# Spectral-mix kernel after sliding-window attention: the last mode's transposed rows by products with stationary weights, another order of the first units, and two weight packs cut into 112 and 8 partitions

## The chip, the core and the metric

The kernel runs on one core of a Trainium2 chip. The metric is device time in microseconds, the median of several runs. Five engines work side by side: PE (TensorE, matrix products; PEld is its weight load), DVE (VectorE), ACT (ScalarE), POOL (GpSimd) and SP (SyncE). Data moves through 16 DMA engines. DMAs that POOL issues form queue q0, those that SP issues form queue q1. What a DMA engine has in one queue it does in the order of issue. A DMA's rows are spread over the DMA engines, and a DMA counts as landed when the last of its engines has reported.

## The reference

```python
def _attn_ref(q, k, v):            # 8 batches, 8 heads, 576 tokens, 64 wide
    scores = scale * q @ k^T + bias (ALiBi slopes), masked to a causal window of 128
    return softmax(scores) @ v
def _moe_ref(x, w_r, w_i, w_ch):   # x: the attention's output as (8, 576, 512)
    X = rfft(x, axis=1); Xr, Xi = first 64 modes
    Yr = Xr @ w_r[m] - Xi @ w_i[m]; Yi = Xr @ w_i[m] + Xi @ w_r[m]
    u = x + irfft(Y, n=576)
    return u + relu(u @ w_ch)
```

The weights w_r and w_i are 64 matrices of 512x512 each in 4-byte floats, 134 MB in all. They are read once and cast to bf16 by the DMA itself.

## The kernel before

**Attention** fills the first 125 us. It leaves the tokens `x`, the spectra `XC` (channels in the partitions) and the table of the inverse transform `FT`.

**Modes.** Work is then ordered by mode. For each mode there are two weight tiles, numbered t = 2m (w_r) and t = 2m+1 (w_i), and each has four slices a of 128 rows. The product at line 886 holds 32 columns of `XC` stationary (8 batches, real and imaginary, with gaps) and lets a weight slice of 512 columns move: out come 32 rows of 512, in a quarter of the PSUM tile `acc`. Four modes are one quad g; g = 15 is the last (`LAST`). Its modes 60 to 62 go to a tile of their own, `part_acc` ("pa" in the profile), and mode 63 goes to the fourth quarter of `acc`.

**Weight stream.** POOL issues the weights (`load_w`, line 472; `load_packs`, line 491) into a ring of buffers, a pack of two tiles at a time: 128 partitions, 1 MB after the cast. The last packs come as single tiles (line 499), and the very last tile, t = 127, in three parts: slices 0 and 1, slice 2, slice 3. POOL's DMAs take turns at eight semaphores; each waits until the DMA eight places before it has landed, and a pack also waits until PE has used the buffer up.

**Beside the stream** PE turns spectra back into token space (`stream_spectra`, `project`, `augment`), at line 934 it runs `warm` products that nobody reads, and in the last quad, at i = 6, it begins unit 0 (`begin`, `channels`, `add_tokens`, `finish_tokens`). A unit is two batches by 128 tokens, or four batches by the last 64 tokens; there are 18.

**After the stream** stands an order written out by hand (lines 951 to 998). ACT scales mode 63's rows into `yq` in two halves (line 960), PE transposes them (962), DVE copies them to `yT` (964), PE multiplies `yT` by `w_ch` into `zl` (601), and ACT casts that to `yw` (603). DMAs then put the rows of quad 15 where the other units read them: `patch` (line 648) copies rows of `yq` to `Z` and of `yw` to `ZW`, per batch, batches 0 and 1 through SP or POOL and the others through POOL, eight rows each or six and two. Unit 0, and the channel half of unit 1, do not wait for these DMAs: they add the last quad's rows by a product with a small matrix `FM` (`last_rows`, line 786). `FM` is filled by two DMAs of 8 rows (line 916), early in the stream, between two packs.

For each unit the PSUM tile `mm` is the channel product, `yy` the tokens plus spectral rows; ACT takes the relu of `mm` (line 802), DVE adds `yy` (line 842; unit 0: lines 816 and 823) and SP stores the result (line 844). Five output buffers rotate.

Lines that the steps touch: 491 (packs), 593/596 (transposed rows of modes 60 to 62), 601/603, 648, 786, 816/823, 842, 886, 916, 955 to 998.

Of the kernel before, what the change touches and what calls it, by code (L numbers as in the profile page):

```python
# [412 lines left out]
def kernel(  # L413
# [46 lines left out]
    turns[1].remove(1)  # L460
    wq, homes, todo_w, again = {}, {}, [i for turn in turns for i in turn], []

    def load_w(n, pool, chosen=None):
# [11 lines left out]
    def load_packs(n, pool):  # L475

        for _ in range(n):
            pack = [i for i in todo_w if i not in again][:2]
            if not pack:
                return  # L480
            assert len(pack) == 2
            t = pool.tile([P, 2, 4, DM], BF16, tag="w", name="w")
            kinds = {i % 2 for i in pack}
            for s, i in enumerate(pack):
                todo_w.remove(i)
                homes[i] = pool if s else False
                wq[i] = [t[:, s, a] for a in range(4)]
            m, w = pack[0] // 2, (moe_w_r, moe_w_i)
            if len(kinds) == 1:
                assert pack[1] == pack[0] + 2  # L490
                nc.gpsimd.dma_start(  # L491
                    out=t.rearrange("p s a e -> p s (a e)"),
                    in_=w[kinds.pop()][m : m + 2].rearrange("m (p a) e -> p m (a e)", a=4))
                continue
            for s, i in enumerate(pack):
                src = w[i % 2][i // 2].rearrange("(p a) e -> p a e", a=4)
                for part in ((slice(0, 4),) if i < 2 * NM - 1
                             else (slice(0, 2), slice(2, 3), slice(3, 4))):
                    nc.gpsimd.dma_start(out=t[:, s, part], in_=src[:, part])
# [70 lines left out]
    with ExitStack() as mctx:  # L570
# [7 lines left out]
        nc.gpsimd.memset(YT[:, 1, :, :, HM - 4 :], 0.0)  # L578
        lctx, pctx = ExitStack(), ExitStack()
        lps = lctx.enter_context(tc.tile_pool(name="lps", bufs=1, side="right", space=PSUM))  # L580
# [17 lines left out]

        def late_channels(zw, yT, yw, c):
            for et in range(4):  # L600
                nc.tensor.matmul(zw[:, c], lhsT=yT[:, et], rhs=wch[:, et, c],
                                 start=(et == 0), stop=(et == 3))
            nc.scalar.copy(yw[:, c], zw[:, c])

# [131 lines left out]
        HALVES = (1, 2, len(units) - 1)  # L736
        mms, yys, rs = {}, {}, {}

# [73 lines left out]

        def with_tokens(o, n):

            last_rows(yys[0][0], 0, heads["yq"], (n,))
            nc.scalar.copy(o[:, n], yys[0][0][:, n])

        def finish_first(o):

            (mm, mm_slot), (_, yy_slot) = mms.pop(0), yys[0]  # L820
            for n in range(2):
                last_rows(mm, 0, heads["yw"], (n,))
                nc.vector.scalar_tensor_tensor(out=o[:, n], in0=mm[:, n], scalar=0.0,
                                               in1=o[:, n], op0=ALU.max, op1=ALU.add)
                nc.sync.dma_start(out=out[n, :P], in_=o[:, n])
                if n == 0:
                    with_tokens(o, 1)
            del yys[0]
            idle.append(mm_slot)
            free.append(yy_slot)  # L830

        def finish(j):

            b, st = units[j]
            if j not in yys:
                take(j)
            add_tokens(j)
            finish_tokens(j)
            (yy, slot), r = yys.pop(j), rs.pop(j)
            o = heads["out"].tile([P, 2, DM], FP32, tag="o", bufs=5, name="o")  # L840
            for c in parts(j):
# [8 lines left out]
                for n in range(c.start, c.stop):  # L850
# [3 lines left out]
                    )  # L854
            free.append(slot)

        quads, side, recycle = [], [], list(again)
        ZW = Z = XW = FM = FC = pairs = wch = w2 = None
        K1 = spot[again[-1]]
        for g in range(NM // 4):  # L860
# [5 lines left out]
            for i in range(8):  # L866
                k = 8 * g + i
                if i == 6 and g == LAST:
# [4 lines left out]
                    idle.append(0)  # L873
                    free.append(0)
                    begin(0)
                    channels(0)
# [4 lines left out]
                for a in range(4):  # L881
                    for t in now:
                        m, ri = t // 2, t % 2
                        c0 = (a // 2 * 2 * NC + 16 * (1 - ri) + a % 2 * 8) * NM + m
                        into = part_acc if g == LAST and m < NM - 1 else acc
# [13 lines left out]
                if k == K1:  # L899
# [14 lines left out]
                    nc.gpsimd.memset(FM, 0.0)  # L914
                    for b in range(2):
                        nc.gpsimd.dma_start(
                            out=FM.rearrange("(k v) b s -> k v b s", v=16)[:, b, b],
                            in_=FT[64 * b + 56 : 64 * b + 64, b, : 2 * P],
                        )
                    FC = right.tile([P, P], BF16, name="FC")  # L920
# [16 lines left out]
            if g < LAST:  # L937
                quads.append(quad_end(acc, g))
                next(quads[0])
            if g == 7:  # L940
                side += [partial(stream_spectra, 0, bp) for bp in range(B // 2)]
# [3 lines left out]
            elif g == LAST - 1:  # L945
# [5 lines left out]
        yq, yT = heads[LAST]  # L951
        zctx = ExitStack()
        zps = zctx.enter_context(tc.tile_pool(name="zps", bufs=1, space=PSUM))
        zl = zps.tile([P, DM], FP32, tag="z0", name="zl")
        nc.tensor.matmul(zl, lhsT=ident, rhs=wch[:, 0], start=True, stop=True)
        sides = (slice(0, DM // 2), slice(DM // 2, DM))
        trs = (lps.tile([P, 4, P], BF16, tag="tr", name="tr"),
               zps.tile([P, 4, P], BF16, tag="z1", name="tr1"))
        for i, c in enumerate(sides):
            nc.scalar.mul(yq[96:, c], acc[96:, c], 2.0 / S)  # L960
            for et in (2 * i, 2 * i + 1):
                nc.tensor.transpose(trs[i][:, et, 96:], yq[96:, et * P : (et + 1) * P],
                                    ident[96:, 96:])
            nc.vector.tensor_copy(yT[:, 2 * i : 2 * i + 2, 96:],
                                  trs[i][:, 2 * i : 2 * i + 2, 96:])
        patch([(nc.sync, 0), (nc.gpsimd, 1)], yq, lambda b: Z[:, b // 2, 1])
        patch([(nc.gpsimd, b) for b in (2, 3, 4, 5, 6)], yq, lambda b: Z[:, b // 2, 1], 6)
        yw = F[:, : DM // (2 * NM)].rearrange("p a b -> p (a b)")
        heads.update(yq=yq, yw=yw)
        first = heads["out"].tile([P, 2, DM], FP32, tag="o", bufs=5, name="o")  # L970
        with_tokens(first, 0)
        for i, c in enumerate(sides):
            zl = zps.tile([P, DM], FP32, tag=f"z{i}", name=f"zl{i}")
            late_channels(zl, yT, yw, c)
        zctx.close()
# [10 lines left out]
        channel_rows = partial(patch, rows=yw, dst=lambda b: ZW[:, b // 2, 1])  # L986
        channel_rows([(nc.sync, 0), (nc.sync, 1)] + [(nc.gpsimd, b) for b in range(2, B)])
        patch([(nc.gpsimd, 7)], yq, lambda b: Z[:, b // 2, 1], 6)

# [3 lines left out]
        finish(1)  # L993
        activate(2)
        for j in range(3, len(units)):
            activate(j)
# [32 lines left out]
```

## Time and profile before

| | us |
|---|---|
| median of 3 runs | 438.93 (438.69 to 439.68) |
| the profiled execution's own time | 437.99 |
| its span, first to last instruction | 436.1 |
| last weight matmul ends (line 886) | 402.8 |
| first output store issued (line 825) | 406.89 |
| last output store issued (line 851) | 430.80 |

| stretch, us from the span's start | what runs |
|---|---|
| 0 to 125 | attention; the first weights |
| 125 to 402.4 | weight stream, a pack each 4.9 us |
| 402.8 to 409.8 | mode 63's way to the first units |
| 409.8 to 436.1 | the remaining units, and their stores |

How to read it: the page gives each engine's busy time; the chain follows the end back from what released what; the timeline lists instructions with the idle time before them in brackets and what ended it. The trace also keeps, for each DMA, the times at which its 16 engines reported, and the start of every packet; where the text speaks of a DMA engine, it speaks of those.

### The profile page before, as it was taken

How to read it: one execution, taken by the hardware profiler on the slowest of the kernel's cores; microseconds unless marked ns; L12 is line 12 of the kernel's file. 1: busy time of each engine (PE TensorE's matmuls, PEld its weight loads, DVE VectorE, ACT ScalarE, POOL GpSimd, SP SyncE). 2: the span in 40 equal slices, each digit the busy share in tenths (PEclk: the TensorE clock that was granted, in tenths of full speed). 3: DMA queues.
4: the chain of work that ended last, by engine and by line, in shares of the span. 5: the costliest groups of instructions: out<-in, count | busy, mean ns of one | idle time of the engine just before them, and what ended most of it. 6: DMA issues, size and time to landing. Idle time of an engine off the chain costs nothing.

```text
span 436.1 us, 8292 instructions
## 1 busy us (share of the span) xinstructions
PE 316.2 (73%) x3488; PEld 177.7 (41%) x3509; DVE 184.5 (42%) x332; ACT 162.3 (37%) x211; POOL 90.2 (21%) x170
## 2 busy tenths in 40 slices
PE   5589899979686635543442487999889999788982
PEld 4367677757565312111111133444434444334430
DVE  7789799887783301000000021322213233122684
ACT  6949899988681000000000011322222322102780
POOL 8701010103424002222112110101111110012600
PEclk9969999999999955555555569999999999989997
DMA  8999999999999999999999999999999999998598
GB/s 285 326 311 310 290 316 300 307 298 299 252 217 212 215 215 213 214 214 214 215 212 214 214 215 214 215 214 215 215 214 214 215 215 215 213 215 153 190 378 311
DMA packets 50453, 105.54 MB, mean 242 GB/s; under 512 B 4032, under 2 KB 21072, under 8 KB 50416
## 3 DMA queue, kind: packets, MB, share of 16 engines
q0 software_dynamic: 19440, 68.41, 77.9%
q1 hardware_dynamic: 30976, 36.60, 25.3%
q8 instruction: 27, 0.44, 0.4%
q14 instruction: 10, 0.08, 0.1%
HBM read 162.53 MB, written 9.44 MB: 394 GB/s over the span
## 4 chain that ended last, share of the span: by engine, by line
DMA 71%; PE 10%; DVE 8%; issue 5%; POOL 2%; ACT 1%; SPq 1%; DVEq 0%; POOLq 0%; ACTq 0%
DMA w<-in_moe_w_i_dram 42%; DMA wch<-in_moe_w_ch_dram 8%; DMA qr<-in_q_dram 7%; DMA vr<-in_v_dram 6%; DVE o L842 3%; DMA qr<-in_moe_w_i_dram 3%; PE my L702 2%; DMA vr<-in_moe_w_r_dram 2%; DMA kr<-in_k_dram 2%; DVE vb L246 1%; PE acc L886 1%; PE av L344 1%; POOL Z L648 1%; PE my L659 1%; DVE att L318 1%
## 5 line engine op out<-in xcount | busy, mean ns | idle before, releaser
L886 PE MATMUL acc<-w,XC 128*32 128x512 bf16 x456 | 80.3, 478 | 68.5 <-DMA w<-in_moe_w_i_dram 34.2
L886 PEld LDWEIGHTS <-XC 128*32 128x32 bf16 x508 | 38.4, 147 | 109.2 <-issue 82.8
L307 ACT ACTIVATE att<-sc 128x1024 bf16<-128x1024 f32 x64 | 64.1, 1032 | 9.7 <-PE sc L297 9.6
L636 ACT CAST ZW<-zw 128x512 bf16<-128x512 f32 x8 | 4.7, 585 | 142.9 <-PE zw L634 142.9
L344 PE MATMUL av<-vb,att 128*128 128x132 bf16 (+1 forms) x576 | 38.4, 217 | 13.3 <-DVE x L360 8.6
L344 PEld LDWEIGHTS <-att 128*128 128x128 bf16 x704 | 36.6, 98 | 18.7 <-DVE x L360 12.0
L608 DVE TENSOR_SCALAR yq<-acc 128x512 bf16<-128x512 f32 x14 | 9.6, 687 | 81.8 <-PE acc L886 81.8
L702 PE MATMUL my<-wch,xT 128*64 128x512 bf16 x288 | 34.5, 381 | 5.7 <-ACT x L733 4.2
L711 ACT CAST XW<-my 128x512 bf16<-128x512 f32 x36 | 19.3, 589 | 50.5 <-PE my L659 50.5
L683 DVE COPY xT<-tr 128x1024 bf16<-128x1024 bf16 x18 | 12.4, 692 | 54.9 <-PE tr L681 54.9
L269 ACT COPY qkT<-tp 128x1152 bf16<-128x1152 bf16 x30 | 33.5, 1116 | 4.1 <-PE tp L263 3.6
L491 POOL DMA_DIRECT2D w<-in_moe_w_r_dram x22 | 15.6, 710 | 72.1 <-PE acc L886 46.1
L491 POOL DMA_DIRECT2D w<-in_moe_w_i_dram x23 | 16.3, 709 | 64.1 <-PE acc L886 45.3
L297 PE MATMUL sc<-qkT 64*64 64x256 bf16 (+2 forms) x640 | 25.1, 263 | 4.8 <-ACT qkT L269 1.2
L360 DVE TENSOR_TENSOR x<-av,rec 128x640 bf16<-128x640 f32 x32 | 26.4, 825 | 1.1
L702 PEld LDWEIGHTS <-xT 128*64 128x64 bf16 x288 | 17.1, 109 | 21.5 <-issue 9.1
L246 DVE CAST vb<-vr 64x1024 bf16<-64x1024 f32 x32 | 22.6, 708 | 0.2
L733 ACT CAST x<-my 128x512 bf16<-128x512 f32 x18 | 10.5, 585 | 31.6 <-PE my L659 31.6
L297 PEld LDWEIGHTS <-qkT 64*64 64x64 bf16 x640 | 14.5, 109 | 19.1 <-issue 16.0
L734 DVE CAST x<-my 128x512 bf16<-128x512 f32 x18 | 12.4, 692 | 21.7 <-PE my L659 21.7
L842 DVE TENSOR_TENSOR o<-yy,r 128x1024 f32<-128x1024 f32 (+1 forms) x20 | 20.3, 1059 | 2.1 <-ACT r L802 1.9
L318 DVE TENSOR_TENSOR att<-att,mask 128x1024 bf16<-128x1024 bf16 x32 | 20.5, 682 | 0.0
(137 smaller groups left out, 424.7 us busy)
## 6 DMA issues: line engine op xcount, KB each, us to landing
w<-in_moe_w_i_dram POOLq DMA_DIRECT2D x23, 1024.0 KB, 36.2
w<-in_moe_w_r_dram POOLq DMA_DIRECT2D x22, 1024.0 KB, 35.6
qr<-in_q_dram SPq DMA_DIRECT2D x16, 576.0 KB, 7.9
kr<-in_k_dram SPq DMA_DIRECT2D x16, 576.0 KB, 7.9
w<-in_moe_w_r_dram POOLq DMA_DIRECT2D x16, 512.0 KB, 14.2
vr<-in_v_dram SPq DMA_DIRECT2D x56, 128.0 KB, 7.6
w<-in_moe_w_i_dram POOLq DMA_DIRECT2D x13, 512.0 KB, 24.0
out_dram<-o SPq DMA_DIRECT2D x13, 512.0 KB, 5.0
```

The costliest lines, as they stand in the source:

```text
L246: nc.vector.tensor_copy(self.vb[u % 2][row, :, :, :, W * half : W * half + D], src[row, :2])
L269: (self.nc.vector.tensor_copy if u < 2 and w == "q" else self.nc.scalar.copy)(dst.rearrange("q h (p j) -> q h p j", j=TPP), tp.rearrange(" ...
L297: nc.tensor.matmul(sc[64 * half : 64 * half + 64, e, j * 256 + c0 : j * 256 + c0 + n], lhsT=qkT[row, 1, h, k0 + j : k0 + P : 2], rhs=qkT[r ...
L307: self.nc.scalar.activation(self.att[u % 2][:, kt * 8 * P : (kt + 1) * 8 * P], sc.rearrange("p e n -> p (e n)"), AF.Exp, scale=1.0 / math. ...
L318: nc.vector.tensor_tensor(out=rows, in0=rows, in1=self.table[:, heads], op=ALU.mult)
L344: nc.tensor.matmul(bank[:, qt * W : qt * W + rhs[j].shape[1]], lhsT=att[:, o : o + P], rhs=rhs[j], start=(n == 0 and j == 0), stop=(n == l ...
L360: nc.vector.tensor_tensor(out=self.x[:, b, :, cs].rearrange("p t (h d) -> p h t d", h=2), in0=tiles[:, :, :, :D], in1=rec.unsqueeze(-1).br ...
L491: nc.gpsimd.dma_start(out=t.rearrange("p s a e -> p s (a e)"), in_=w[kinds.pop()][m : m + 2].rearrange("m (p a) e -> p m (a e)", a=4))
L702: nc.tensor.matmul(mm[ROWS[half]], lhsT=lhsT, rhs=wch[:, dt], start=(dt == 0), stop=False, skip_group_check=True,)
L711: nc.scalar.copy(XW[:, j, n], mms[n])
L842: nc.vector.tensor_tensor(out=o[:, c], in0=yy[:, c], in1=r[:, c], op=ALU.add)
L886: nc.tensor.matmul(into[32 * (m % 4) : 32 * (m % 4) + 32], lhsT=XC[:, c0 : c0 + 31 * NM + 1 : NM], rhs=wq[t][a], start=(ri == 0 and a == 0 ...
```

## The change

Three parts.

1. **Transposed rows.** The new `last_columns` computes, for mode 63, the transposed rows directly: each 128x128 block of a weight slice is stationary, 32 columns of `XC` move, and the sum over both tiles and four slices stands in the PSUM tile `lastT`. It is called ahead of each product of line 886 of mode 63, so that there are 8 times 4 such products. ACT's scaling into two halves, PE's transposes and two DVE copies after the stream give way to one DVE operation on `lastT` and one ACT scaling of all 512 columns.
2. **Order of the first units.** The casts to `yw` go from ACT to DVE. Both halves of unit 0's token rows are added after `zl`, and both halves of its channel rows before DVE reads the first. Unit 2's tokens are computed before unit 3's channel product. POOL issues the patches of batches 2 to 7 in pairs, token rows and channel rows in turn; one product that read `wch` into an unused `zl` is gone.
3. **FM and two packs.** The two DMAs that filled `FM` become four of 8 rows by 128 columns. They are issued inside two w_r packs (the next of one kind after quads 8 and 10): such a pack comes as 112 partitions, then 8 partitions, an `FM` DMA, 8 partitions, an `FM` DMA.

```diff
@@ load_packs
-                nc.gpsimd.dma_start(
-                    out=t.rearrange("p s a e -> p s (a e)"),
-                    in_=w[kinds.pop()][m : m + 2].rearrange("m (p a) e -> p m (a e)", a=4))
+                into = t.rearrange("p s a e -> p s (a e)")
+                src = w[kinds.pop()][m : m + 2].rearrange("m (p a) e -> p m (a e)", a=4)
+                done = 16 if between else 0
+                nc.gpsimd.dma_start(out=into[done:], in_=src[done:])
+                for o in range(0, done, 8):
+                    nc.gpsimd.dma_start(out=into[o : o + 8], in_=src[o : o + 8])
+                    between.pop(0)()
@@
+        def last_columns(t, a):
+            m, ri = t // 2, t % 2
+            c0 = (a // 2 * 2 * NC + 16 * (1 - ri) + a % 2 * 8) * NM + m
             for et in range(4):
-                nc.tensor.matmul(zw[:, c], lhsT=yT[:, et], rhs=wch[:, et, c],
-                                 start=(et == 0), stop=(et == 3))
-            nc.scalar.copy(yw[:, c], zw[:, c])
+                nc.tensor.matmul(
+                    lastT[:, et], lhsT=wq[t][a][:, et * P : (et + 1) * P],
+                    rhs=XC[:, c0 : c0 + 31 * NM + 1 : NM],
+                    start=(ri == 0 and a == 0 and et == 0), stop=(ri == 1 and a == 3),
+                    skip_group_check=True,
+                )
@@ finish_first
+            last_rows(mm, 0, heads["yw"])
             for n in range(2):
-                last_rows(mm, 0, heads["yw"], (n,))
                 nc.vector.scalar_tensor_tensor(out=o[:, n], in0=mm[:, n], scalar=0.0,
                                                in1=o[:, n], op0=ALU.max, op1=ALU.add)
                 nc.sync.dma_start(out=out[n, :P], in_=o[:, n])
-                if n == 0:
-                    with_tokens(o, 1)
@@
+        def mode_rows(b, c):
+            nc.gpsimd.dma_start(out=FM.rearrange("(k v) b s -> k v b s", v=16)[:, b, b, c],
+                                in_=FT[64 * b + 56 : 64 * b + 64, b, c])
@@ the loop over t in now
+                        if m == NM - 1:
+                            last_columns(t, a)
@@
-                    for b in range(2):
-                        nc.gpsimd.dma_start(
-                            out=FM.rearrange("(k v) b s -> k v b s", v=16)[:, b, b],
-                            in_=FT[64 * b + 56 : 64 * b + 64, b, : 2 * P],
-                        )
@@
+            if g in (8, 10):
+                between += [partial(mode_rows, g // 2 - 4, slice(P * h, P * h + P))
+                            for h in range(2)]
@@ after the stream
-        for i, c in enumerate(sides):
-            nc.scalar.mul(yq[96:, c], acc[96:, c], 2.0 / S)
-            for et in (2 * i, 2 * i + 1):
-                nc.tensor.transpose(trs[i][:, et, 96:], yq[96:, et * P : (et + 1) * P],
-                                    ident[96:, 96:])
-            nc.vector.tensor_copy(yT[:, 2 * i : 2 * i + 2, 96:],
-                                  trs[i][:, 2 * i : 2 * i + 2, 96:])
+        nc.vector.tensor_scalar_mul(yT[:, :, 96:], lastT, 2.0 / S)
+        nc.scalar.mul(yq[96:], acc[96:], 2.0 / S)
...
+            for et in range(4):
+                nc.tensor.matmul(zl[:, c], lhsT=yT[:, et], rhs=wch[:, et, c],
+                                 start=(et == 0), stop=(et == 3))
+            nc.vector.tensor_copy(yw[:, c], zl[:, c])
+        with_tokens(first)
...
-        channel_rows([(nc.sync, 0), (nc.sync, 1)] + [(nc.gpsimd, b) for b in range(2, B)])
-        patch([(nc.gpsimd, 7)], yq, lambda b: Z[:, b // 2, 1], 6)
+        channel_rows([(nc.sync, 0), (nc.sync, 1), (nc.gpsimd, 2), (nc.gpsimd, 3)])
+        for b in range(4, B, 2):
+            both = [(nc.gpsimd, b), (nc.gpsimd, b + 1)]
+            token_rows(both)
+            channel_rows(both)
...
         activate(2)
+        tokens_of(2)
         for j in range(3, len(units)):
```

More of the change, by code (lines that the diff above doesn't have):

```diff
@@ L461 @@
     wq, homes, todo_w, again = {}, {}, [i for turn in turns for i in turn], []
+    between = []
     def load_w(n, pool, chosen=None):
@@ L578 @@
         nc.gpsimd.memset(YT[:, 1, :, :, HM - 4 :], 0.0)
-        lctx, pctx = ExitStack(), ExitStack()
+        lctx, pctx, zctx = ExitStack(), ExitStack(), ExitStack()
         lps = lctx.enter_context(tc.tile_pool(name="lps", bufs=1, side="right", space=PSUM))
@@ L597, in late_end @@
             heads[LAST] = yq, yT
-        def late_channels(zw, yT, yw, c):
+        def last_columns(t, a):
+            m, ri = t // 2, t % 2
+            c0 = (a // 2 * 2 * NC + 16 * (1 - ri) + a % 2 * 8) * NM + m
             for et in range(4):
-                nc.tensor.matmul(zw[:, c], lhsT=yT[:, et], rhs=wch[:, et, c],
-                                 start=(et == 0), stop=(et == 3))
-            nc.scalar.copy(yw[:, c], zw[:, c])
+                nc.tensor.matmul(
[4 more added lines that the diff above has]
+                )
         def quad_end(acc, g):
@@ L736 @@
         HALVES = (1, 2, len(units) - 1)
-        mms, yys, rs = {}, {}, {}
+        mms, yys, rs, summed = {}, {}, {}, set()
         def pair(tag, slot=0):
@@ L811, in finish_tokens, with with_tokens @@
             late_modes(yys[j][0], j, Z)
-        def with_tokens(o, n):
-            last_rows(yys[0][0], 0, heads["yq"], (n,))
-            nc.scalar.copy(o[:, n], yys[0][0][:, n])
+        def with_tokens(o):
+            last_rows(yys[0][0], 0, heads["yq"])
+            for n in range(2):
+                nc.scalar.copy(o[:, n], yys[0][0][:, n])
         def finish_first(o):
             (mm, mm_slot), (_, yy_slot) = mms.pop(0), yys[0]
+            last_rows(mm, 0, heads["yw"])
             for n in range(2):
-                last_rows(mm, 0, heads["yw"], (n,))
                 nc.vector.scalar_tensor_tensor(out=o[:, n], in0=mm[:, n], scalar=0.0,
@@ L830, in finish_first, with tokens_of @@
             free.append(yy_slot)
-        def finish(j):
-            b, st = units[j]
+        def tokens_of(j):
             if j not in yys:
@@ L838, in finish @@
             finish_tokens(j)
+            summed.add(j)
+        def finish(j):
+            b, st = units[j]
+            if j not in summed:
+                tokens_of(j)
             (yy, slot), r = yys.pop(j), rs.pop(j)
@@ L874 @@
                     free.append(0)
+                    zps = zctx.enter_context(tc.tile_pool(name="zps", bufs=1, space=PSUM))
+                    lastT = zps.tile([P, 4, 32], FP32, tag="z1", name="lastT")
                     begin(0)
@@ L951 @@
         yq, yT = heads[LAST]
[L952 to L955, printed above, removed]
         sides = (slice(0, DM // 2), slice(DM // 2, DM))
-        trs = (lps.tile([P, 4, P], BF16, tag="tr", name="tr"),
-               zps.tile([P, 4, P], BF16, tag="z1", name="tr1"))
-        for i, c in enumerate(sides):
-            nc.scalar.mul(yq[96:, c], acc[96:, c], 2.0 / S)
-            for et in (2 * i, 2 * i + 1):
-                nc.tensor.transpose(trs[i][:, et, 96:], yq[96:, et * P : (et + 1) * P],
-                                    ident[96:, 96:])
-            nc.vector.tensor_copy(yT[:, 2 * i : 2 * i + 2, 96:],
-                                  trs[i][:, 2 * i : 2 * i + 2, 96:])
+        nc.vector.tensor_scalar_mul(yT[:, :, 96:], lastT, 2.0 / S)
+        nc.scalar.mul(yq[96:], acc[96:], 2.0 / S)
         patch([(nc.sync, 0), (nc.gpsimd, 1)], yq, lambda b: Z[:, b // 2, 1])
-        patch([(nc.gpsimd, b) for b in (2, 3, 4, 5, 6)], yq, lambda b: Z[:, b // 2, 1], 6)
+        token_rows = partial(patch, rows=yq, dst=lambda b: Z[:, b // 2, 1], lo=6)
+        token_rows([(nc.gpsimd, 2), (nc.gpsimd, 3)])
         yw = F[:, : DM // (2 * NM)].rearrange("p a b -> p (a b)")
@@ L970 @@
         first = heads["out"].tile([P, 2, DM], FP32, tag="o", bufs=5, name="o")
-        with_tokens(first, 0)
         for i, c in enumerate(sides):
             zl = zps.tile([P, DM], FP32, tag=f"z{i}", name=f"zl{i}")
-            late_channels(zl, yT, yw, c)
+            for et in range(4):
[3 more added lines that the diff above has]
+        with_tokens(first)
         zctx.close()
```

## The prediction, as it went on record

> **What bounds the kernel.** I read the chain of the page first, then the windows by stage, then the timeline of the end, then the trace's landings.
>
> ```profile
> q8 instruction: 27, 0.44, 0.4%
> ...
> DMA 71%; PE 10%; DVE 8%; issue 5%; POOL 2%; ACT 1%; SPq 1%; DVEq 0%; POOLq 0%; ACTq 0%
> ```
>
> The chain is DMA for 71%. From 125 to 402.4 us this is the weight stream. The first line, from the list of queues, looks harmless: 27 fetches of 16 KB of code. They matter below.
>
> ```profile
> core 0: us, PE busy (x) PEld busy (x) DVE busy (x) ACT busy (x) POOL busy (x), PEclk, DMA share, GB/s
> 140.00:399.00 259.00, 180.51 (x1280) 80.46 (x1278) 49.36 (x106) 34.55 (x62) 40.67 (x66) 0.79 1.06 214
> ...
> 402.80:409.80 7.00, 5.74 (x62) 2.75 (x67) 3.07 (x7) 4.77 (x11) 5.99 (x12) 1.00 0.28 89
> 409.80:430.20 20.40, 16.73 (x214) 7.20 (x211) 18.96 (x18) 14.62 (x16) 0.74 (x2) 1.00 1.00 368
> ```
>
> Three stages, read in the last two columns: the stream (DMA engines always busy), 7.0 us in which they stand nearly idle (0.28), and the units, in which output stores fill them again (1.00) and DVE is busy for 18.96 of 20.4 us. So the time is the end of the stream, plus the way from there to the first units, plus units and stores, which move as one block. The change touches the first two.
>
> The timeline at the seam:
>
> ```profile
> 400.10 1.08 PE L886 MATMUL acc<-w,XC 128*32 128x512 bf16 x4
> 401.11 0.34 PE L593 MATMUL tr<-ident,yq 96*128 96x96 bf16 x4
> 401.39 0.86 PE L886 MATMUL acc<-w,XC 128*32 128x512 bf16 x3
> 402.42 0.38 PE L886 MATMUL acc<-w,XC 128*32 128x512 bf16 x1 [0.17 <-DMA w<-in_moe_w_i_dram]
> 402.88 0.65 ACT L960 ACTIVATE yq<-acc 32x256 bf16<-32x256 f32 x2 [5.04 <-PE acc L886]
> 403.31 0.48 PE L962 MATMUL tr<-ident,yq 32*128 32x32 bf16 x4 [0.52 <-ACT yq L960]
> 403.56 0.51 DVE L964 COPY xT<-tr 128x64 bf16<-128x64 bf16 x2 [1.70 <-PE tr L962]
> 403.95 1.04 PE L601 MATMUL zl<-wch,xT 128*128 128x256 bf16 x8
> 404.63 0.76 ACT L603 CAST F<-zl 128x256 bf16<-128x256 f32 x2
> 405.61 1.22 SPq L648 DMA_DIRECT2D ZW<-F  x2
> 409.79 7.09 DVE L842 TENSOR_TENSOR o<-yy,r 128x512 f32<-128x512 f32 x7 [0.38 <-ACT r L802]
> ```
>
> From 400.10 PE hardly rests: it waits 0.17 us for the last weights. `yw` is whole at 405.39 (404.63 + 0.76); SP sends its rows to `ZW` at 405.61; DVE's unbroken row of units begins with unit 2 at 409.79.
>
> **Part 3, the packs.** A pack takes 4.89 us on each DMA engine, which carries 8 of its 128 partitions: 0.61 us a partition. The landings tell that the 16 engines do not end together. Microseconds after the first engine:
>
> ```
> wch (first 227.53):       0 .07 .10 .16 .17 .40 .41 .79 | 1.22 1.24 1.65 1.77 1.82 2.19 2.20 2.25
> last weights (399.08):    0 .15 .17 .40 .40 .41 .63 .78 | 2.29 2.32 2.71 2.85 2.88 3.26 3.27 3.30
> FM, 1st DMA (227.17):     0 .13 .14 .17 .22 .46           1.25 2.20
> FM, 2nd DMA (same zero):  .49 .87                         1.26 1.67 1.82 1.85 2.24 2.29
> ```
>
> Eight engines are early, eight late, and the stream ends with the latest. Following the offsets from DMA to DMA, each 16 KB code fetch between 211 and 393 us (nine) sets one of the late eight back by another 1.1 us, and none of the early eight. An engine's packets keep their spacing (0.154 us per 2 KB) when the early ones are through: each has its own pace, so work moved from one to another moves its end.
>
> The lower two rows are the starts of FM's packets. An 8-row DMA uses 8 engines, the next one the other 8. The first took six early engines and two late ones, with offsets 1.25 and 2.20; I follow these two to about 2.3 and 3.27 at the end. In the order of the changed kernel on POOL a split pack reads 112, 8, FM, 8, FM. The 112 give 7 partitions to each engine. If 8-row DMAs alternate as in this trace, both weight pieces fall on one half and both FM pieces, which cost next to nothing, on the other: the one half carries 9 partitions, the other 7. Two split packs: +1.22 us and -1.22 us. The first 8-row DMA is now a weight piece, so it takes the half that the first FM transfer took; its late engine ends at 3.27 + 1.22 = 4.49 after the first engine's old end, where the latest was 3.30. **The stream ends 1.2 us later.** With the other half it would be 3.30 + 1.22, the same. Bounds: -1.2 if the half were exactly the early eight, 0 if pieces spread over all 16, +1.2.
>
> The Trainium skill (DMA: Bandwidth & Descriptors, "Why a DMA increments its semaphore by 16 and not by 1") gives a transfer of few rows to consecutive engines from a round-robin cursor. The two FM rows agree; the first two six-row patches at 400.5 and 401.1 do not, since both used the same five early engines.
>
> The six more DMAs on POOL cost about 0.53 us of issue each (row L499), beside a POOL that waits 91 us for PE in the stream. They also take places among the eight semaphores. Counting these, the pack after the first split waits for a pack three places ahead: at least three packs, 14.7 us, stay queued, so no DMA engine runs dry. Without that cover each us of delay would be one of the stream. FM lands some 60 us before its first use.
>
> **Part 1, PE.** Eight groups of four products with 128x128 stationary and 32 moving columns are added in front of eight products that PE does almost without rest. No row shows this pair of shapes in turn. A pair of load and product: L962, with 32 columns, starts each 40 ns (403.31, 403.35); L344, with full weights and 66 columns, each 30 ns. Switching between the 32-column stationary of line 886 and full weights: 400.80 to 401.11 is 0.31 us after a product that takes 0.215, and 401.25 to 401.39 is 0.14 after one of 0.045; 0.095 us each way. So a slice costs 4 x 0.04 + 0.095 + 0.215 + 0.095 = 0.565 us. Bounds: 0.335 if switches vanish and pairs take 30 ns; 0.73 if the switch costs half as much again and the long product 0.27, as it does first in a row. I take 0.565, since both its rows have these shapes.
>
> From 400.10, without part 3: tile 126 to 402.36; transposes of line 593, 0.18, to 402.54; slices 0 to 2 of tile 127 to 404.24; the last four small products start until 404.36, and DVE can begin 0.21 later (403.35 to 403.56), at 404.57. The weights, landed by 402.37, no longer matter: PE has become the bound here. DVE scales 128 columns in 0.24 (between 0.19 for 64 and 0.36 for 384): 404.81. `zl` from 404.91, eight products of 0.11, ends 405.51 and 405.95; DVE casts each half in 0.39 (ACT: 0.38): `yw` whole at 406.38, against 405.39. That is **+1.0 us** (bounds -0.7 and +2.3). What goes (ACT's halves, transposes, copies: 402.88 to 404.07) is paid for by more than it cost.
>
> By the page TensorE: Matmul & The Clock Gate, "LDWEIGHTS", of the Trainium skill, loading 128 columns takes 128/1.2 = 107 ns; 32 pairs at that price would take 3.4 us in place of my 1.3, and the sum below would be 2.1 us more. L344's 30 ns speak against it.
>
> **Part 2, the order.** SP sends `ZW` 0.22 after `yw` as before. The second SP DMA landed at 408.03, 2.64 after `yw`; that gives 409.0. The work ahead shifts too: `yq` in one piece (0.58 after the last product) holds unit 0's token rows until 405.8, PE reaches unit 0's channel rows at 406.9, DVE's two L823 steps run 407.35 to 408.65 with no gap (before: 405.90, 407.13). Then unit 2's channel product at 409.0, and at once its tokens, which before stood behind unit 3's channel product (unit 2's product at 408.09, tokens from 409.06). DVE starts unit 2 at 410.1 and unit 3 at 411.45, against 409.79 and 410.99: the order **gives back 0.5 us** of the 1.0. POOL's interleaved patches for batches 2 and 3 land at about 410.1; unit 4 needs them later than that. If they came late, each 0.5 us issue would be one of delay for unit 4 alone.
>
> **The sum.** +1.2 (stream) + 1.0 (`yw`) - 0.5 (order) = +1.7 us on 437.99, the profiled execution's own time (span 436.1 and 1.9 around it): 439.7. That execution is 0.94 below the median shown, so on the median the forecast is 438.93 + 1.7 = 440.6.
>
> **Rivals.**
> - *The pieces fall on the early eight*, and the change is **faster**. For it: the two groups stand 2.4 us apart at the end, just what two split packs move (2 x 1.22). Against it: the FM rows put two late engines in one half and six in the other. It decides as soon as all eight engines of the pieces end below 2.08. Price -1.2 in place of +1.2: 438.93 - 1.2 + 0.5 = 438.2; with PE's lower bound 436.5. Chance 0.14.
> - *The pieces spread over all 16, or change sides between the packs*, so that part 3 does not do what it is cut for: 438.93 + 0.5 = 439.4. No row of weights in 8 partitions speaks to it. Chance 0.16.
> - *The added products hide.* Pieces as forecast, but PE at its lower bound, so that `yw` is 0.7 earlier: 438.93 + 1.2 - 0.7 - 0.5 = 438.9. For it: L344's 30 ns. Against it: the two switches. Chance 0.12.
> - The forecast, 440.6, with 439.9 to 442.4 by PE's upper bound and the order: 0.58.
>
> Range: 438.0 to 442.2. It leaves out the lower half of the first rival and the top of the forecast's PE bound. A measurement here can tell about 0.2% (0.88 us) from no change. Faster than 438.05: most of the first rival's lower half and a little of the third, 0.13. Slower than 439.81: the forecast but 0.03 of it, and a part of the second and third, 0.64. Within: 0.23.
>
> **What would show it.** Part 3: the spread between the first and last engine of the last weight DMA, 3.30 before, about 5.3 by the forecast (-0.81 to 4.49), about 1.0 by the first rival (1.07 to 2.08); last weights landing near 403.6 or 401.2. Part 1: line 886 and the new product alternating from about 401.3 with no DMA wait, about 0.57 us a slice. Part 2: unit 2's DVE step some 3.7 us after `yw` (before 4.4). If the slices wait for DMA instead, PE is not the bound and the price is wrong; if DVE's units do not start as a block after unit 2, part 2 is.

## The result, and the profile after

The changed kernel takes 442.59 us in the median of six runs (440.89 to 444.27), the kernel before 438.81 (438.23 to 439.68) beside it: a ratio of 1.0080, 95% interval 1.0056 to 1.0104, which is 2.5 to 4.6 us slower. Forecast were 440.6 and a range up to 442.2. The direction was right, the size was not: +1.7 forecast, +3.8 measured. The profiled execution took 442.24 (span 440.5), 4.25 more than the one of before.

From the page of the changed kernel, the code fetches and the chain:

```profile
q8 instruction: 27, 0.44, 0.4%
...
DMA 74%; PE 10%; DVE 7%; issue 4%; ACT 2%; SPq 1%; POOL 1%; DVEq 0%; ACTq 0%; POOLq 0%
```

The chain looks as before. The windows show the difference (columns as before, the last three are the granted clock, the DMA share and GB/s):

```profile
140.00:399.00 259.00, 176.46 (x1279) 80.73 (x1280) 49.45 (x107) 33.98 (x62) 43.82 (x72) 0.81 1.07 214
401.90:407.60 5.70, 5.70 (x48) 2.99 (x44) 0.62 (x2) 0.00 (x0) 2.35 (x5) 1.00 0.09 16
407.60:413.50 5.90, 5.25 (x54) 2.36 (x55) 3.37 (x7) 3.57 (x7) 4.94 (x10) 1.00 0.30 100
413.50:434.40 20.90, 16.90 (x217) 7.45 (x215) 19.21 (x19) 15.00 (x17) 1.97 (x4) 1.00 0.97 354
```

A new stage stands between stream and units: 5.70 us in which PE is busy throughout and the DMA engines are nearly idle (0.09). The last weights landed at 404.16 and PE's last product on them ends at 407.60; in the kernel before these were 402.37 and 402.79. The weights are there and PE is not through with them.

The seam, from the timeline of the changed kernel (PE's products, and the first step of each engine after them; brackets hold the idle time before a row and what ended it):

```profile
401.89 0.39 PE L609 MATMUL lastT<-XC,w 128*128 128x32 bf16 x4
402.21 0.43 PE L910 MATMUL acc<-w,XC 128*32 128x512 bf16 x1
402.57 0.39 PE L609 MATMUL lastT<-XC,w 128*128 128x32 bf16 x4
...
406.85 0.39 PE L609 MATMUL lastT<-XC,w 128*128 128x32 bf16 x4
407.17 0.43 PE L910 MATMUL acc<-w,XC 128*32 128x512 bf16 x1
407.33 0.29 DVE L975 TENSOR_SCALAR xT<-lastT 128x128 bf16<-128x128 f32 x1 [1.98 <-PE lastT L609]
407.68 1.05 PE L986 MATMUL zl<-wch,xT 128*128 128x256 bf16 x8
408.33 0.86 DVE L988 CAST F<-zl 128x256 bf16<-128x256 f32 x2 [0.70 <-PE zl L986]
409.33 0.39 PE L670 MATMUL mm<-ZW,FT 64*64 64x512 bf16 x4
409.75 1.22 SPq L659 DMA_DIRECT2D ZW<-F  x2
411.80 0.40 PE L670 MATMUL yy<-Z,FT 64*64 64x512 bf16 x2 [0.57 <-DMA Z<-yq]
412.68 3.83 ACT L813 ACTIVATE r<-mm 128x512 f32<-128x512 f32 x5 [0.87 <-PE mm L670]
413.81 0.41 PE L773 MATMUL mm<-XW,ident 64*64 64x512 bf16 x4 [0.31 <-ACT r L813]
414.99 1.23 DVE L858 TENSOR_TENSOR o<-yy,r 128x1024 f32<-128x1024 f32 x1 [0.20 <-PE yy L670]
```

A slice is the step from one `lastT` row to the next: 0.68 us (401.89, 402.57). `yw` is whole at 409.19 (408.33 + 0.86), unit 3's step on DVE starts at 414.99. With the landings of the trace, the 4.25 us split without remainder:

| us | before | after | more |
|---|---|---|---|
| tile 126 landed | 399.85 | 401.62 | 1.77 |
| from there to its first product | 0.25 | 0.27 | 0.02 |
| from that to `yw` whole | 5.29 | 7.30 | 2.01 |
| from `yw` to unit 3 on DVE | 5.60 | 5.80 | 0.20 |
| from there to the end of the execution | 27.00 | 27.25 | 0.25 |

### The profile page after: what moved, and what is told of

Read it like the earlier page. It is cut to its first block, busy times and chain, and to the rows that moved or that the text cites. A ratio compares the mean times of both kernels' runs of the same rounds, so it can differ in the third digit from the quotient of the medians.

```text
span 440.5 us, 8370 instructions
## 1 busy us (share of the span) xinstructions
PE 318.3 (72%) x3536; PEld 179.4 (41%) x3536; DVE 185.5 (42%) x333; ACT 161.4 (37%) x208; POOL 93.5 (21%) x176
## 4 chain that ended last, share of the span: by engine, by line
DMA 74%; PE 10%; DVE 7%; issue 4%; ACT 2%; SPq 1%; POOL 1%; DVEq 0%; ACTq 0%; POOLq 0%
DMA w<-in_moe_w_r_dram 36%; DMA w<-in_moe_w_i_dram 19%; DMA qr<-in_q_dram 7%; DMA vr<-in_v_dram 7%; DMA kr<-in_k_dram 3%; PE av L344 2%; DVE vb L246 2%; DVE att L318 1%; DMA out_dram<-o 1%; DVE o L858 1%; PE acc L910 1%; POOL w L495 1%; ACT att L307 1%; PE my L713 1%; DVE x L360 1%
## 5 line engine op out<-in xcount | busy, mean ns | idle before, releaser
L910 PEld LDWEIGHTS <-XC 128*32 128x32 bf16 x508 | 39.3, 147 | 109.6 <-issue 83.7
L284 PE MATMUL sc<-bias,ident 128*128 128x512 bf16 x64 | 20.3, 402 | 1.1 <-ACT att L307 1.1
```

What stands on the lines that cost most here:

```text
L284: nc.tensor.matmul(sc[:, e], lhsT=self.ident, rhs=self.bias[:, hv].rearrange("p j n -> p (j n)"), start=True, stop=False, skip_group_check ...
L910: nc.tensor.matmul(into[32 * (m % 4) : 32 * (m % 4) + 32], lhsT=XC[:, c0 : c0 + 31 * NM + 1 : NM], rhs=wq[t][a], start=(ri == 0 and a == 0 ...
```

## The experiments

Each was timed in five rounds beside the kernel before; "more" is against that, with the ratio's interval turned into us. "Without part 3" is the kernel of e2.

### The three parts by themselves: e1 to e4

e1 is the kernel before with the cut packs and FM's pieces of the diff above and nothing else; e2 the changed kernel with whole packs and FM's two early DMAs; e3 the kernel before with `last_columns` and, in place of ACT's halves, line 962's transposes and two DVE copies,

```diff
+        nc.vector.tensor_scalar_mul(yT[:, :, 96:], lastT, 2.0 / S)
+        nc.scalar.mul(yq[96:], acc[96:], 2.0 / S)
```

and without the product into the unused `zl`; e4 is the kernel before with the other hunks: casts on DVE, `with_tokens` after `zl`, `tokens_of(2)`, the patches in pairs.

> The kernel before with part 3 alone: the two cut packs with FM's pieces between them. Theory, pieces pile up: both weight pieces of a cut pack go through the same half of the DMA engines, so the spread between the first and the last engine at the last weights is about 4.5 us (3.30 before), the last weights land 1.2 to 1.8 us later, and the time is 1.2 to 1.8 us above the kernel before. Rival, pieces harmless: the later end of the stream in the profile of the changed kernel was one execution's scatter; the spread stays at 3.3 and the time within 0.4 us.

> The changed kernel without part 3: whole packs, FM filled by two DMAs early in the stream as before; parts 1 and 2 stay. Theory: PE is the bound at the end of the stream and the order gives nothing back, so the time is 1.8 to 2.2 us above the kernel before. Rival, as predicted: slices cost 0.565 us and the order gives back 0.5, so 0.5 us above. Rival, all in the packs: no difference to the kernel before.

> The kernel before with part 1 alone: lastT by added products, one DVE and one ACT scaling in place of halves, transposes and copies; the order after the stream stays as before. Theory: eight slices of 0.68 us, so yw is whole 2.0 us later, and perhaps 0.7 more because ACT has unit 0's first token copy ahead of the casts to yw: 2.0 to 2.7 us above the kernel before. Rival, slices of 0.565 us: 1.0 above.

> The kernel before with part 2 alone: casts to yw on DVE, unit 0's halves together, unit 2's tokens ahead of unit 3's channel product, patches in pairs. Theory: no gain, since the tokens of unit 1 wait for the patch of batch 1 in front of what was moved ahead: within 0.4 us of the kernel before. Rival, as predicted: 0.5 us faster.

| | median, us | ratio, 95% | more, us |
|---|---|---|---|
| e1, part 3 alone | 438.88 | 1.0014 (0.9991 to 1.0037) | 0.6 (-0.4 to 1.6) |
| e2, parts 1 and 2 | 441.29 | 1.0069 (1.0052 to 1.0086) | 3.0 (2.3 to 3.8) |
| e3, part 1 alone | 442.39 | 1.0096 (1.0073 to 1.0118) | 4.2 (3.2 to 5.2) |
| e4, part 2 alone | 438.84 | 1.0009 (0.9997 to 1.0021) | 0.4 (-0.1 to 0.9) |

Most of the loss lies in part 1 (the forecast for parts 1 and 2 together was 0.5). e2 excludes both rivals, but lies above the theory's 1.8 to 2.2 as well. Its seam is that of the changed kernel: 7.30 us from the first product to `yw`, 5.73 from there to unit 3, together 2.14 more than before. The rest of its 3.0, some 0.9, the seam does not account for. e3 lies above its 2.0 to 2.7; its clock is taken up below. Part 2 by itself brings nothing, but e3 and e4 together lose more (4.6) than e2, so behind part 1 the new order is better than the old one. e1 falls between theory and rival and is taken up below.

### What a slice costs: e5 and e8

e5, without part 3, puts the 16 added products of a tile together; e8 leaves the eight products of line 886 for mode 63 out and turns `yT` back instead:

```diff
@@ e5
-                        if m == NM - 1:
-                            last_columns(t, a)
+                        if m == NM - 1 and a == 0:
+                            for part in range(4):
+                                last_columns(t, part)
@@ e8
                             last_columns(t, a)
+                            continue
@@ e8, after yT is scaled
+        for et in range(4):
+            nc.tensor.matmul(acc[96:, et * P : (et + 1) * P], lhsT=yT[:, et, 96:], rhs=ident,
+                             start=True, stop=True, skip_group_check=True,
+                             tile_position=(0, 96))
+        nc.scalar.copy(yq[96:], acc[96:])
```

> The changed kernel without part 3 (441.29 us), but the 16 added products of a tile come together, ahead of its four products of line 886, in place of four ahead of each. Theory, the switches cost: a slice of 0.68 us is three steps of 0.05, 0.16 from the last small product to the long one and 0.36 from the long one to the next small one, so that 0.1 and 0.145 of it are the two switches; a tile then takes about 2.1 us in place of 2.72, lastT is whole some 2 us earlier, yq and zl follow the last product of line 886 about 1.3 us earlier, and the time is 1.2 to 1.4 us less, about 440.0. Rival, loading full weights is the price: each added product costs the same wherever it stands, and the time stays at 441.3.

> The changed kernel without part 3, and mode 63 without its eight products of line 886: only the added products stand there, and the rows of yq come from yT by four products with the identity, ahead of zl, and an ACT copy. It computes the same output. Theory, PE stops to be the bound: a tile takes about 1.0 us, the last four products follow the last weights (about 402.7) at once, yT is scaled by 403.4, zl ends about 404.7 and yw is whole about 405.2, 2.6 us earlier than in the changed kernel without part 3 and 0.2 to 0.5 earlier than before: 438.0 to 438.6, at best just below the kernel before. Rival, the added products themselves are the price, not their mixing with line 886: 440 or more.

e5: 439.11 us, ratio 1.0020 (1.0000 to 1.0039), 0.9 more; by the medians 2.2 less than e2. The timeline of e5 shows how PE's time went:

```profile
402.03 1.09 PE L604 MATMUL lastT<-XC,w 128*128 128x32 bf16 x16
403.05 1.08 PE L902 MATMUL acc<-w,XC 128*32 128x512 bf16 x4
404.06 0.34 PE L593 MATMUL tr<-ident,yq 96*128 96x96 bf16 x4
404.24 1.08 PE L604 MATMUL lastT<-XC,w 128*128 128x32 bf16 x16
405.25 1.08 PE L902 MATMUL acc<-w,XC 128*32 128x512 bf16 x4
405.42 0.29 DVE L969 TENSOR_SCALAR xT<-lastT 128x128 bf16<-128x128 f32 x1 [0.62 <-PE lastT L604]
```

Sixteen small products with the switch after them take 1.02 us (402.03 to 403.05), so 0.06 each; four long ones with a switch take 1.01. A tile is 2.03 us where the interleaved one is 2.72 (4 x 0.68). What fell away, 0.69 us a tile, is three switches each way and the longer time of the first long product in a row. First product to `yw`: 5.74 us, against 7.30. The switches were the price of the 1.6 us between them, and the theory is right in this.

In the profiled execution part of the gain is lost again: from `yw` to unit 3 it takes 6.43 us (e2: 5.73). One engine reports SP's second `ZW` patch 0.71 us behind the others, at 411.40, and two of PE's four products on `ZW` wait for it until 411.44:

```profile
411.03 0.81 PE L665 MATMUL mm<-ZW,FT 64*64 64x512 bf16 x4
```

A code fetch had begun at 408.12; that it held up this engine is likely, but the trace does not name engines. The gain in the median, 2.2, is more than the 1.2 to 1.4 expected and, with the scatter of both, not at odds with it.

e8: 439.72, 1.0026 (1.0006 to 1.0046), 1.1 more, where at most 0.2 was expected. It lies between theory and rival. In its profiled execution PE no longer bounds, it waits 0.26 us for the last slice; but its clock fell, as it did in e3.

### The clock after a pause: e10 and e11

The kernel before has a product into an unused `zl` at 402.72, between the last weights and the transposes; it is gone in e3, e8 and the changed kernel. In e3 PE then stands still for 0.7 us. Windows of e3:

```profile
403.60:407.00 3.40, 2.67 (x22) 1.38 (x20) 0.65 (x2) 0.59 (x1) 0.00 (x0) 1.00 0.00 0
407.00:410.40 3.40, 3.40 (x18) 1.45 (x18) 0.00 (x0) 1.33 (x3) 3.17 (x7) 0.50 0.04 7
410.40:413.00 2.60, 1.82 (x16) 0.65 (x16) 1.45 (x3) 1.28 (x3) 2.60 (x6) 1.00 0.12 21
```

After 3.4 us in which PE was busy for 2.67, the clock is 0.50 for 3.4 us, and with it each of the products on the way to `yw` and `ZW` takes up to twice as long. The Trainium skill (TensorE: Matmul & The Clock Gate, "Part 1: The HAM clock gate (the "warmup" mystery)") has the half clock come after an idle window of about 3.4 us. The length agrees with these rows; that a whole window must be idle does not, here PE was busy for 2.67 us of it. Nor is the pause alone what lowers the clock. The kernel before has the same busy time in one stretch of that length, and its clock is 1.00 there and until 431.7:

```profile
400.97:404.38 3.41, 2.67 (x18) 1.49 (x19) 0.74 (x3) 0.88 (x3) 2.07 (x6) 1.00 0.17 28
```

What differs is what the products moved: by the shapes in the trace some 2500 columns in e3's stretch (2600 in e8's), 4100 in this one. Whether that decides was not tested.

e10 is e3, e11 is e8 with

```diff
+        for _ in range(3):                                  # e11: 2
+            zl = zps.tile([P, DM], FP32, tag="z0", name="zl")
+            nc.tensor.matmul(zl, lhsT=ident, rhs=wch[:, 0], start=True, stop=True)
         nc.vector.tensor_scalar_mul(yT[:, :, 96:], lastT, 2.0 / S)
```

> The kernel of e3 (part 1 alone, 442.39 us; it also lost the product into the unused zl) with three products that nobody reads after the last product of line 886. Theory: in e3 PE stood idle for 0.7 us at 406.3 to 407.0 and its granted clock fell to 0.50 from 407 to 410.3, so that zl took 1.9 us in place of 1.05; kept busy, PE stays at 1.00, yw is whole about 1 us earlier and the time is 1 to 1.5 us less, about 441.0 to 441.4. Rival: the low clock was one execution's chance or not on the path; the time stays near 442.4.

> The kernel of e8 (mode 63 by the added products alone, rows of yq turned back; 439.72 us) with two products that nobody reads after the last added product. Theory: in e8 PE's clock fell to 0.50 from about 407.9 to 411.2 after pauses of 0.26 and 0.44 us; with the second pause filled it stays at 1.00, yw is whole 2.6 to 2.8 us after the last weights in place of 3.1, and the time is 1 to 1.5 us less, 438.3 to 438.7. Rival: the pause while PE waits for the last slice is enough to lower the clock; no gain.

The same windows of e10:

```profile
403.60:407.00 3.40, 3.29 (x21) 1.47 (x21) 0.29 (x1) 0.59 (x1) 0.29 (x1) 1.00 0.00 0
407.00:410.40 3.40, 2.83 (x22) 1.22 (x20) 0.93 (x2) 1.82 (x4) 3.40 (x8) 1.00 0.08 15
```

The clock stays at 1.00, and in e11 too: products to `yw` take 5.12 us there, 5.39 in e8. The times are 441.87 (1.0084, 1.0054 to 1.0114) and 439.10 (1.0014, 0.9998 to 1.0030): 0.5 and 0.6 us less than e3 and e8, less than expected, with intervals that overlap. That the clock stays up in the two profiled executions with the pause filled is shown; what it is worth in the median stays open, since only the profiled executions show these stretches. In that of the changed kernel it is 1.00 in all these windows: this is no part of the 4.25 us above.

e10 tells one more thing. With the old order behind part 1, first product to `yw` takes 8.39 us, against 7.30 with the new order: `zl` then waits on PE behind unit 0's token rows, which wait for ACT's scaling in one piece. The products that nobody reads have a share in it: the third starts at 406.55, when the scaled rows have been there since 406.42. Part 2 saves most of this wait. Behind `yw` it saves nothing against the kernel before (5.73 us to unit 3 in e2, 5.60 before).

### Why the order gives nothing back: e7 and e9

In the changed kernel the patch of batch 1's token rows, issued at 408.56, lands at 411.76, because one DMA engine reports 1.5 us behind the other fifteen: PE's code fetch at 409.29 hits it. Unit 1's tokens wait for it (411.80 in the timeline above). e7, without part 3, moves the fetch by unread products in the stream; e9 also moves unit 0's token rows:

```diff
@@ e7
+        extra = [5] * 5
         def warm():
-            for _ in range(3):
+            for _ in range(3 + (extra.pop() if extra else 0)):
@@ e9
-        with_tokens(first)
         zctx.close()
...
         channels(1)
+        with_tokens(first)
```

> The changed kernel without part 3 (441.29 us), with 25 more of the products that nobody reads, put where PE waits for weights (376 to 399 us), so that PE's code fetch of 16 KB near the end comes some 25 pairs of load and product earlier, before the patches after the stream. Theory, in the changed kernel this fetch (408.24 to 409.22 without part 3) sets one DMA engine back just when it carries the patch of batch 1's token rows, and unit 1's tokens wait for it: the patch lands 1.7 us after its issue in place of 3.06, unit 2's relu starts 3.1 us after yw in place of 3.42, and the time is 0.3 to 0.5 us less. Rival, the patch is not on the path: no difference, with the landing earlier or not.

> The kernel of e7 (parts 1 and 2, code fetch moved; 441.46 us) with unit 0's token rows added after unit 1's channel product instead of before it. Theory: SP's ZW patch is not released by yw but by unit 1's channel product, which reads ZW (408.27 there, 0.56 after yw; the product starts its last four at about 407.85); the two products yy<-yq, which part 2 moved between zl and that product, push it back. Without them in front SP sends ZW 0.1 to 0.2 after yw, unit 2's relu starts about 2.9 to 3.0 after yw in place of 3.42, and the time is 0.4 to 0.5 us less, about 441.0. Rival: SP waits for DVE's casts, which report later than ACT's; then SP still sends 0.56 after yw and nothing is gained.

e7: 441.46, 1.0060 (1.0041 to 1.0078). The fetch came at 404.23 and the patch landed at 408.78, 1.70 us after its issue (e2: 3.06), as expected; unit 1's DVE step began 2.37 us after `yw` (2.97), but unit 2's relu 3.42 after it, just as in e2. The rival is right: this patch is not on the path to unit 2.

e9: 440.98, 1.0056 (1.0034 to 1.0078), again within the noise of e2. From its timeline:

```profile
407.61 0.39 PE L665 MATMUL mm<-ZW,FT 64*64 64x512 bf16 x4
...
408.02 1.23 SPq L654 DMA_DIRECT2D ZW<-F  x2
...
410.53 0.41 PE L770 MATMUL mm<-XW,ident 64*64 64x512 bf16 x4 [0.58 <-DVE o L832]
```

SP now sends `ZW` 0.12 us after `yw` (407.90), where e2, e4, e7 and the changed kernel have 0.56. So SP's patch waits for unit 1's channel product, which must have read `ZW` before it is overwritten, and part 2 had put unit 0's token rows ahead of that product. In the kernel before, that product had ended just ahead of SP's patch at 405.61:

```profile
405.15 0.39 PE L659 MATMUL mm<-ZW,FT 64*64 64x512 bf16 x4
```

That half of the theory holds. Little of the gain follows: SP's second patch, though sent 0.44 earlier than in e7 as counted from `yw`, was longer on its way (2.00 us, e7: 1.72) and lands 2.79 us after `yw` (e7: 2.93). And unit 2's channel product cannot begin before 410.53 in any case, since until then DVE's second step of unit 0 reads the PSUM place that it takes. The relu starts 3.30 after `yw` (e7: 3.42). Two waits end within 0.2 us of each other, so that taking one away uncovers the other.

One row of numbers holds in all these traces: unit 2's relu starts 0.48 to 0.54 us after SP's second patch has landed, in the kernel before (landed 2.64 after `yw`), the changed one (2.94), e2 (2.93), e4 (3.22), e5 (3.63), e7 and e9.

### The cut packs: e6, e13 and e14

e6 is the changed kernel, e14 is e13, with FM's pieces behind both weight pieces; e13 is e1 with cuts from quad 6 on:

```diff
@@ e6, e14
                 for o in range(0, done, 8):
                     nc.gpsimd.dma_start(out=into[o : o + 8], in_=src[o : o + 8])
+                for o in range(0, done, 8):
                     between.pop(0)()
@@ e13, e14
-            if g in (8, 10):
+            if g in (6, 8, 10, 12):
```

> The changed kernel with FM's two pieces of a cut pack issued after both weight pieces, so that 8-row transfers in a row read weights, weights, FM, FM. Theory, one half of the DMA engines carries both weight pieces and FM's pieces only because they alternate: now each half carries one of each, the spread between the first and the last engine does not grow at the two cut packs, and the time is 1.2 us below the changed kernel, the same as without part 3 (441.3). Rival, the six more DMAs themselves cost: 442.6 as in the changed kernel.

> The kernel before with four packs cut as in part 3 in place of two (FM's four transfers are written a second time for it). Theory, the half is fixed within an execution and adds up: 1.22 us a pair of packs, so that the spread at the last weights grows to 5.5 to 6.5 us, the last weights land about 2.4 us later and the time is 2.0 to 2.6 us above the kernel before. Rival, the side changes between packs or from execution to execution: the time is 0.3 to 1.2 us above, with a wide scatter.

> The kernel of e13, but with FM's two transfers behind both weight pieces of each cut pack. Theory: each half of the DMA engines carries one weight piece of a pack, the spread stays as in the kernel before and the time is within 0.5 us of it. Rival, the twelve more DMAs or the cutting cost by themselves: the same as e13.

The landings of e13 and e14 hold three cut packs, not four: after quad 12 no pack of one kind was left to cut. Times: e6 440.61 (1.0049, 1.0032 to 1.0066; 2.1 more), e13 439.51 (1.0012, 0.9993 to 1.0032; 0.5 more), e14 438.76 (1.0013, 0.9992 to 1.0033; 0.6 more). So e13's theory failed and its rival holds, and e14 is at the edge of its 0.5. e6 lies 2.0 under the changed kernel, but also 0.7 under e2, which has no cuts at all, so differences of this size say little. The medians of e13 and e14 cannot tell the two orders apart. The landings can. In the kernels without cuts, the last engine ends the stream 172.59 to 172.66 us after it ended `wch`, in all eleven profiled executions, the kernel before among them; so the end can be foretold from `wch`, and what a cut adds is the rest:

| | cuts | spread at `wch`, us | spread at last weights | stream's end over `wch` + 172.62 |
|---|---|---|---|---|
| before | 0 | 2.25 | 3.30 | -0.03 |
| e2, without part 3 | 0 | 1.73 | 2.76 | -0.02 |
| e6, both halves | 2 | 3.09 | 4.09 | +0.06 |
| e14, both halves | 3 | 3.21 | 4.28 | +0.16 |
| after | 2 | 1.45 | 4.46 | +0.92 |
| e1 | 2 | 3.02 | 4.32 | -0.32 |
| e13 | 3 | 2.97 | 6.27 | +0.96 |

Where each half gets one piece, the spread grows by 1.0 to 1.1, as without cuts. Where FM's pieces alternate with the weights it grows by 3.0 and 3.3, the pile-up of the forecast, but in e1 only by 1.3. The landings do not name the engines, but only one assignment leaves the offsets of half of them unchanged. By it the pile-up is plain in the changed kernel (offsets from the first engine; the pack before the second cut, the pack after it):

```
both pieces:  1.08 1.12 1.18 1.45 1.48 1.69 2.15 2.17  ->  2.29 2.32 2.41 2.73 2.76 2.91 3.37 4.44
no piece:     0    .17  1.07 1.09 1.13 1.27 2.37 2.43  ->  0    .15  1.06 1.10 1.11 1.25 2.34 2.46
```

Eight engines are set back by 1.2 (one of them by a code fetch as well), eight not at all. But in e1 the latest engine at the first cut (offset 3.59) was among those with no piece, and the stream ended 0.3 us earlier than without the cuts. Which engines are late differs from execution to execution, and so does the price.

### A version with both remedies: e12

e12 is e11 with `with_tokens` moved as in e9.

> The kernel of e11 with unit 0's token rows behind unit 1's channel product as in e9. Both theories together: yw 2.7 us after the last weights, SP sends ZW at once, unit 2's relu starts 5.6 to 5.8 us after the last weights (6.2 in the kernel before), and the time is 0.3 to 0.6 us under the kernel before, about 438.1. Rival: one of the two theories fails, and the time is that of the kernel before or above it.

439.30 us, ratio 1.0007 (0.9987 to 1.0027): no different from the kernel before, better than the changed one. First product to `yw` is 5.13 us (before 5.29) and unit 2's relu starts 6.16 us after the last weights (before 6.18). The rival holds: the gain in PE's stage, 0.16 us by these rows, does not reach the unit.

## Why the prediction was wrong, step by step

- **"So a slice costs 4 x 0.04 + 0.095 + 0.215 + 0.095 = 0.565 us": this term failed, by size.** PE is the bound as forecast, with no DMA wait between the slices. But a slice takes 0.68: small products start 0.04, 0.06 and 0.06 apart, the long one 0.16 after the last of them, the next small one 0.36 after that. With the small one at 0.06 and the long one at 0.27 this leaves 0.10 and 0.09 for the two switches. Those, at 0.095, were right. Too low were the small product (0.04, from L962, whose stationary has 32 rows) and the long one: 0.215 holds in a row of its kind, 0.27 for the first in a row, and here every long product is a first one. That value stood in the upper bound, 0.73 (the terms named there add up to 0.715), where it did no work. Seven whole slices stand in front of the last four small products. They make 0.82 us, and with 0.20 in the steps behind (0.48 from the last slice's first product to DVE, forecast 0.33; DVE's scaling 0.29, forecast 0.24) first product to `yw` took 7.30 instead of 6.28.
- The estimate of 107 ns for a load of 128 columns, by the rule of the Trainium skill (TensorE: Matmul & The Clock Gate, "LDWEIGHTS (loading the stationary operand)"), does not agree: 16 pairs in a row took 0.06 us each in e5.
- **"The order gives back 0.5 us": this step failed.** From `yw` to unit 3 it is 5.80 us, forecast 5.07, before 5.60. Two things were overlooked, both readable in the trace of before. "SP sends `ZW` 0.22 after `yw` as before" took the patch to wait for `yw`; it waits for unit 1's channel product (before: last four from 405.15 for 0.39, SP at 405.61), and the token rows were moved in front of that. And unit 3's tokens still stand behind unit 4's channel product, which waits for unit 2's relu to end (413.81 in the timeline above): from that relu's start to unit 3 it is 2.31 us in the changed kernel, e2, e4 and e7, and 2.45 before. My unit 3 at 411.45 had left this wait out. Together: SP's second patch lands 2.94 after `yw` (before 2.64), unit 2's relu starts 0.54 after that (0.51), unit 3 starts 2.31 after the relu (2.45). Of the 0.5 the new order gave back 0.14, and the later patch cost 0.30.
- **"The stream ends 1.2 us later": right in its mechanism, too large on average.** The pile-up on one half is there, with 1.2 us per engine for two packs. The stream's end pays it only if the latest engine is in that half: +0.92, -0.32 and +0.96 (for three packs) in the three profiled executions. The forecast followed two late engines of one execution and took them for fixed. Spread at the last weights was 4.46, between the forecast's 5.3 and before. The other 0.8 us of the 1.77 were there at `wch` already (last engine 230.62, before 229.78), ahead of any cut.
- The rivals: "the added products hide" is refuted by the seam, "the pieces fall on the early eight" by the changed kernel's landings, "change sides" describes part 3 best, but its time, 439.4, lies further from the result than the forecast, since the loss is in parts 1 and 2.
- What would show it: "about 0.57 us a slice" and "unit 2's DVE step some 3.7 us after `yw`" (4.32) both showed the steps wrong. With the sizes measured in this one execution the sum is 0.9 (stream) + 2.0 + 0.2 + 0.25 = 3.4, within the interval of 2.5 to 4.6.

What is not settled: the 0.25 us in the units and stores; the some 0.9 us by which e2's median exceeds its seam; and the part of part 3 in the median, which no comparison here resolves better than about 1 us.

## What to carry to other kernels

Extra products on an engine that is about to become the bound should be grouped by the shape of their stationary operand: the same products cost 1.6 us less in e5 than alternating. When an instruction is moved ahead, look for the writes that must wait until a later reader on that engine is done; when such a wait has always been short, the timeline shows it only as two rows that end and begin together (405.54 and 405.61 here). A pack cut into pieces should hand each group of DMA engines the same number of them; the landings show why, the medians do not resolve it.

## What the runs showed of the hardware that was not expected

- The stream is very regular: from the mean of the engines' landings of `wch` to that of the last weights it was 172.13 or 172.14 us in all eleven profiled executions without cuts, while its start moved by up to 5.8 us (first engine's `wch` at 226.02 to 231.84). In these executions the scatter of the stream's end is made before `wch`, by the start and by how far the late engines are behind.
- After 3.4 us in which PE was busy for 2.7, its clock was 0.50 for the next 3.4 us in e3 and e8; with two or three products that nobody reads in the pause it stayed at 1.00. The pause alone is not the rule: the kernel before has 2.67 busy in 3.41 us and keeps 1.00.
- A code fetch of 16 KB (1.0 to 1.4 us) that meets a small patch makes it land 1.4 us later: 3.06 us after issue (e2) in place of 1.70 (e7).
- Four products of 512 columns and sixteen of 32 took 2.72 us of PE when the two kinds alternated and 2.03 when each kind stood together (e2 and the changed kernel, e5): a switch between the two shapes of stationary operand is some 0.1 us each way.
